# Two token groups share weight slices in rounds of seven, five and four instead of ten and six

## The chip, the cores and the metric

The kernel runs on one core of a Trainium2 chip. The metric is device time in microseconds (us), the median of several runs. A profile is one more execution, recorded by the hardware profiler; its span runs from the first to the last instruction. The engines are PE (matrix products), ACT (activations and copies with a scale), DVE (elementwise work and reductions), POOL (elementwise work) and SP, which here only issues DMAs. Each engine takes its own instructions in the order in which the program gives them.

## The reference

```python
k_p = k.reshape(B, H, Sp, 8, D).mean(axis=3)          # B 8, H 8, S 576, D 64, Sp 72
v_p = v.reshape(B, H, Sp, 8, D).mean(axis=3)
scores = np.matmul(q, k_p.transpose(0, 1, 3, 2)) / np.sqrt(D)
attn = softmax(scores)                                # max, exp, sum, as usual
x = np.matmul(attn, v_p)                              # as 4608 tokens of 512 channels
h = x @ w_in1                                         # 512 x 2048
x1 = (h * sigmoid(h)) @ w_out1                        # 2048 x 512
h = x1 @ w_in2
out = (h * clip(h + 3, 0, 6) / 6) @ w_out2
```

The weights come in double precision, as pairs of 32-bit words.

## The kernel before

**Groups and slices.** The 4608 tokens are 36 tiles of 128; four tiles make a group, so there are nine groups. The first weight matrix is cut into 16 slices of 128 hidden columns. A *slot* of the main loop (line 1008) is one product of a group with a slice (`h_mm`, line 628): 12 matmuls of 512 columns, three for each of four blocks, since a weight and an x value are each kept as a rounded head and a tail. The list `order` (line 837) says which group and slice a slot takes: slots 0 to 9 are group 0 with slices 0 to 9, slots 10 to 19 group 1 with the same slices, slots 20 to 25 and 26 to 31 the two groups with slices 10 to 15. From slot 32 on each group runs through all 16.

**Slices.** A slice's raw words are loaded by SP (line 119) and converted in four steps: *scale* on ACT (line 126), *bits*, three DVE instructions (lines 133, 136, 140), *head* on ACT (line 147), *tail* on DVE (line 152). The table `stages` says in which slot each step stands.

**Attention.** Group 0's tiles 0 to 3 are done ahead of slot 0. For a later tile the table `todo` places the steps: *scores* (PE, line 458, into two PSUM banks), *maxima* (DVE, lines 502 and 505), *exponentials* (ACT, line 512, eight of them, which also sum), *norm* (DVE, lines 529, 532, 533), then for group 1 *transposes* on PE (line 544) with two ACT copies out of PSUM (line 545), *weighted* (PE, line 592) and *split* of the result into head (ACT, line 608) and tail (DVE, line 609), which is the group's x. From group 2 on the transpose is three DVE instructions (line 566) and DMAs. In slots 0 to 9 group 1's tiles 4 to 7 pass through these steps, a tile every two slots, while one slice a slot is converted.

**The gate.** After a slot's product comes `silu`: tanh on ACT (line 641) and one DVE instruction (line 642), both in the next slot. Its store is issued by SP a slot later. The product's PSUM bank is free after it; `h_mm` takes turns over four banks, two of a pool `ps_h` and two called y0 and y1.

**Keys and values.** Batches 2 and up are loaded (lines 368, 376) in slots of their own (`kv_in`, from slot 6 on) and summed in eights by POOL. `summed_v` does this on PE (line 395) for two pairs of batch 1 in slots 0 and 1.

Of the kernel before, what the change touches and what calls it, by code (L numbers as in the profile page):

```python
# [27 lines left out]
def kernel(  # L28
# [14 lines left out]
    nc = tc.nc  # L43
# [78 lines left out]
    def split_scale(f):  # L122

        hw = w_raw[f][:, :, 1]
        mag = w_mag[f] = prep_tile("out", DM)
        nc.scalar.activation(mag, hw.bitcast(F32), AF.Copy, scale=2.0 ** -112)

    def split_bits(f):


        raw = w_raw.pop(f)
        bits = w_mag[f].bitcast(U32)
        nc.vector.tensor_scalar(
            out=bits, in0=bits, scalar1=3, scalar2=None, op0=ALU.logical_shift_left
        )
# [12 lines left out]

    def split_tail(f):

        t = w_sl[f]
        nc.vector.tensor_tensor(
            out=t[:, 1, :], in0=w_mag.pop(f), in1=t[:, 0, :].bitcast(F32), op=ALU.subtract
        )
        t = t.rearrange("p a (c f) -> p a c f", f=P)
        w_sl[f] = (t[:, 0], t[:, 1])
# [462 lines left out]
    def h_mm(g, f, m):  # L619
        ih, il = w_sl[f]  # L620
        xh, xl = xs[g]
        if m % 2:
            ps = ps_y.tile([P, GT], F32, tag=f"y{m // 2 % 2}", name="hps")
        else:
            ps = ps_h.tile([P, GT], F32, tag="h", name="hps")
        for n, (w, x) in enumerate(((ih, xh), (il, xh), (ih, xl))):
            for c in range(NKC):
                nc.tensor.matmul(  # L628
                    ps,
                    w[:, c, :],  # L630
                    shuffled(x[:, c, :]),
                    start=(c == 0 and n == 0),
                    stop=(c == NKC - 1 and n == 2),
                )
        return ps
# [197 lines left out]
            first_tile.setdefault(b, t)  # L833


    FIRST = 10
    order = [(0, f) for f in range(FIRST)] + [(1, f) for f in range(FIRST)]
    order += [(0, f) for f in range(FIRST, NF)] + [(1, f) for f in range(FIRST, NF)]
    order += [(g, f) for g in range(2, NG) for f in range(NF)]

    todo = {}
# [1 line left out]
    for t in range(TPG, NTILE):  # L843
        g, i = divmod(t, TPG)
        if g == 1:
            s, w = ((-1, 3), (1, 5), (3, 7), (5, 8))[i]
        elif g == 2:
            s, w = ((14, 25), (16, 26), (18, 28), (20, 29))[i]
        else:
            w = NF * (g - 1) + (4, 7, 10, 13)[i]  # L850
            s = w - 10
        start[t] = s
        jobs = [(s, "scores"), (s + 1, "soft"), (w, "weighted"), (w + 1, "split")]
        if g == 1:
            jobs += [(s + 2, "norm"), (s + 3, "probs" if i < TPG - 1 else "early")]
        else:
            jobs += [(s + 3, "norm"), (s + 3, "turn")]
        for n, what in jobs:
            if n >= 0:
                todo.setdefault(n, []).append((what, t))  # L860
# [4 lines left out]
            assert n not in kv_in  # L865
            kv_in[n] = (b, j)
    stages = {}
    for f in range(3, NF):
        n = f if f < FIRST else FIRST + 5 + 2 * (f - FIRST)
        for i, what in ((n - 5, "scale"), (n - 4, "bits"), (n - 3, "head")):  # L870
            if i >= 0:
                stages.setdefault(i, []).append((what, f))

    with tc.manual_schedule():
# [12 lines left out]
        def load_ahead(n):  # L887
            for _ in range(n):
                if ahead:
                    load_w(ahead.pop(0))  # L890
# [31 lines left out]
        for j in range(2, NPAIR):  # L922
            pool_v(1, j)
        load_q(TPG + 1)
        load_ahead(4)
        for t in range(2):
            scores(t, banks[t], 0)
        vps = bank(banks[3], 1)
# [46 lines left out]
        split_bits(1)  # L975
        split_scale(2)
        split_head(1)
        split_bits(2)
        split_tail(1)
        split_scale(3)  # L980
        split_head(2)
        split_bits(3)
        split_tail(2)
        split_scale(4)
        load_ahead(6)

        BEGIN = 20
# [17 lines left out]

        late_silu = []
        pv = {}
        for n, (g, f) in enumerate(order):
            if (g, f) == (NG - 1, 0):
                early.close()  # L1010
                open_ring()
            load_ahead(2)
            if n == 0:
                load_q(TPG + 2)
            if n >= BEGIN - 3:
                load_halves()
            if n in kv_in:
                load_k(*kv_in[n])
                load_v(*kv_in[n])
            for job in due.pop(n, ()):  # L1020
                job()
            while later:
                later.pop(0)()
            now = todo.get(n, ())
            if n == 0:
                ps = h_mm(g, f, n)
                scores(TPG)
            for what, t in now:
                if what == "split" and t < 2 * TPG:
                    split_x(t, pv.pop(t))  # L1030
                elif what == "norm" and t == 2 * TPG - 1:
                    norm(t, 2)
            for what, t in now:
                if what == "soft":
                    all_max(t)
            if late_silu:
                silu(*late_silu.pop())
            for what, t in now:
                if what == "split" and t >= 2 * TPG:
                    split_x(t, pv.pop(t))  # L1040
            for what, i in stages.get(n, ()):
                if what == "head":
                    split_head(i)
            for what, i in stages.get(n, ()):
                if what == "bits":
                    split_bits(i)
            for what, i in stages.get(n, ()):
                if what == "scale":
                    split_scale(i)
            resting = n == BEGIN + 3 if n < 2 * NF else n % NF in REST and n < (NG - 2) * NF  # L1050
            job = jobs.pop(0) if n >= BEGIN and not resting and jobs else None
            if job:
                job[0](job[2])
            for what, t in now:
                if what == "soft":
                    new_pr(t)
                    all_exps(t)
                elif what == "early":
                    probs_T(t, [(ps_y, "y2"), (ps_y, "y3")])
            if n:  # L1060
                ps = h_mm(g, f, n)
            late_silu.append((g, f, n, ps))
            if n == 0:
                vps = bank(banks[3], 1)
            if n < 2:
                summed_v(vps, 1, n)
            if n == 1:
                nc.scalar.activation(vp[1][:, :4 * D], vps[:SP, :4 * D], AF.Copy)
            for what, t in now:
                if what == "scores":  # L1070
                    scores(t)
                    if TPG < t + 2 < NTILE and t > TPG:
                        load_q(t + 2)
                elif what == "weighted":
                    pv[t] = weighted(t, A if t in (TPG + 2, TPG + 3) else [(ps_y, f"y{2 + t % 2}")])
            for what, t in now:
                if what == "norm" and t != 2 * TPG - 1:
                    norm(t, 2)
                elif what == "turn":
                    vector_T(t, n)  # L1080
                elif what == "probs":
                    probs_T(t, [(ps_y, "y2"), (ps_y, "y3")])
            for what, i in stages.get(n, ()):
                if what == "head":
                    split_tail(i)
            if job:
                job[1](job[2])
            if n - 3 in kv_in:
                pool_k(*kv_in[n - 3], nc.gpsimd)
                pool_v(*kv_in[n - 3])  # L1090
            if g == NG - 2 and f in (8, 10):
                next_wide(1)
            if g == NG - 1:
                if f < 2:
# [310 lines left out]
```

## Time and profile before

| | |
|---|---|
| median of 3 runs | 1515.35 us (1514.25 to 1515.46) |
| profiled execution | 1515.26 us, span 1513.5 us |
| PE busy | 1488.4 us, 98% of the span |
| DVE busy | 1239.5 us, 82% |
| ACT busy | 799.1 us, 53% |
| granted TensorE clock, mean | 0.996 of full speed |

PE is busy nearly throughout, so what can change is the rest, about 25 us in which it is idle, and the stretches in which its clock is halved.

### The profile page before, as it was taken

The numbers are of one execution on the slowest core, as the hardware profiler recorded it, in microseconds if no ns is written. First come the engines' busy times: TensorE is split into PE (matmuls) and PEld (weight loads), VectorE is DVE, ScalarE is ACT, GpSimd is POOL, SyncE is SP. The second block draws the span as 40 slices with busy tenths as digits, with TensorE's granted clock in tenths as the row PEclk, the third lists the DMA queues.
The fourth block names the chain that finished last, engine by engine and source line by source line (L and its number), as shares of the span: only waits on it lengthen the run. The fifth ranks groups of instructions, "written<-read, shape, count | busy, mean of one in ns | idle before, by whom it ended". The sixth has DMA issues, their size and how long they took to land.

```text
span 1513.5 us, 30723 instructions
## 1 busy us (share of the span) xinstructions
PE 1488.4 (98%) x11578; PEld 1418.1 (94%) x11578; DVE 1239.5 (82%) x1869; ACT 799.1 (53%) x1779; POOL 342.0 (23%) x389
## 2 busy tenths in 40 slices
PE   8899999999999999999999999999999999999998
PEld 7688888888888999999999999999999999999998
DVE  8879887888775898888988598888885877777776
ACT  5655564556544544444443566777676444444443
POOL 6163443443011000000000244555540000000000
PEclk9999999999999999999999999999999999999999
DMA  9567999899799955555559766556579954444440
GB/s 305 185 189 240 302 302 286 251 296 297 255 310 363 368 184 183 184 177 183 182 175 356 262 216 209 190 198 214 198 249 319 370 167 143 143 142 141 142 137 29
DMA packets 225460, 342.16 MB, mean 226 GB/s; under 512 B 16800, under 2 KB 157984, under 8 KB 225312
## 3 DMA queue, kind: packets, MB, share of 16 engines
q1 hardware_dynamic: 225312, 340.20, 67.6%
q8 instruction: 91, 1.49, 0.4%
q14 instruction: 57, 0.47, 0.1%
HBM read 194.90 MB, written 145.23 MB: 225 GB/s over the span
## 4 chain that ended last, share of the span: by engine, by line
PE 86%; DMA 6%; DVE 5%; issue 1%; ACT 1%; POOL 1%; SPq 0%; DVEq 0%; POOLq 0%; ACTq 0%
PE pl L821 22%; PE pl L805 22%; PE hps L628 20%; PE py L721 11%; PE pa L721 5%; PE ph L721 3%; DMA wraw<-in_moe_w_in_dram 2%; PE aps L592 2%; PE aps L458 2%; DMA stage<-in_v_dram 2%; DVE rs L1244 1%; DMA wst<-ws 1%; DMA x<-rs 1%; ACT pr L512 0%; DVE rw L218 0%
## 5 line engine op out<-in xcount | busy, mean ns | idle before, releaser
L628 PE MATMUL hps<-rx,whl 128*128 128x512 f32 x1728 | 389.7, 384 | 2.9 <-ACT rx L608 1.4
L628 PEld LDWEIGHTS hps<-rx,whl 128*128 128x128 f32 x1728 | 323.9, 190 | 51.5 <-issue 2.6
L805 PEld LDWEIGHTS pl<-rx,wst 128*128 128x128 f32 x3024 | 337.8, 192 | 0.1
L805 PE MATMUL pl<-rx,wst 128*128 128x256 f32 x3024 | 337.8, 275 | 0.0
L821 PE MATMUL pl<-wst,rx 128*128 128x256 f32 x3024 | 337.8, 275 | 0.0
L821 PEld LDWEIGHTS pl<-wst,rx 128*128 128x128 f32 x3024 | 337.8, 192 | 0.0
L223 POOL TENSOR_TENSOR rw<-rw 128x256 f32<-128x256 f32 x96 | 74.3, 781 | 577.6 <-DVE rw L218 555.1
L721 PE MATMUL py<-rx,wst 128*128 128x288 f32 x1152 | 152.5, 287 | 3.5 <-ACT rs L1308 1.9
L721 PEld LDWEIGHTS py<-rx,wst 128*128 128x128 f32 x1152 | 145.8, 190 | 4.1 <-ACT rs L1308 2.1
L642 DVE SCALAR_TENSOR_TENSOR rs<-rs,hps 128x512 f32<-128x512 f32 x144 | 97.7, 680 | 60.0 <-ACT rs L641 59.7
L791 ACT ACTIVATE rx<-ro 128x1024 fp32r<-128x1024 f32 x86 | 90.3, 1059 | 87.6 <-PE pl L805 35.7
L1121 DVE TENSOR_TENSOR rs<-rs,pl 128x512 f32<-128x512 f32 x90 | 61.7, 686 | 69.5 <-PE pl L821 47.2
L792 DVE TENSOR_TENSOR rx<-ro,rx 128x1024 fp32r<-128x1024 f32 x86 | 103.5, 1224 | 14.8 <-ACT rx L791 14.6
L512 ACT ACTIVATE pr<-aps,mxa 128x72 f32<-128x72 f32 x256 | 77.9, 331 | 55.8 <-DVE mxa L505 55.7
L641 ACT ACTIVATE rs<-hps 128x512 f32<-128x512 f32 x144 | 86.5, 610 | 39.2 <-PE hps L628 39.1
L1124 ACT ACTIVATE rs<-pl 128x512 f32<-128x512 f32 x36 | 21.5, 598 | 145.9 <-PE pl L821 76.2
L791 ACT ACTIVATE rx<-ra 128x1024 fp32r<-128x1024 f32 x70 | 73.4, 1059 | 47.3 <-PE pl L805 18.6
L214 ACT ACTIVATE rw<-rw 128x256 fp32r<-128x256 f32 x152 | 62.2, 419 | 64.9 <-POOL rw L223 31.7
L695 POOL TENSOR_TENSOR rx<-ro,rx 128x576 fp32r<-128x576 f32 x39 | 61.3, 1575 | 137.5 <-ACT rx L690 137.5
L792 DVE TENSOR_TENSOR rx<-ra,rx 128x1024 fp32r<-128x1024 f32 x70 | 83.4, 1219 | 9.9 <-ACT rx L791 9.8
L791 ACT ACTIVATE rx<-rb 128x1024 fp32r<-128x1024 f32 x63 | 66.1, 1058 | 44.7 <-PE pl L821 20.5
L218 DVE TENSOR_TENSOR rw<-rw 128x256 fp32r<-128x256 f32 x152 | 74.1, 497 | 10.6 <-ACT rw L214 10.3
(135 smaller groups left out, 2153.7 us busy)
## 6 DMA issues: line engine op xcount, KB each, us to landing
ws<-rw SPq DMA_DIRECT2D x152, 256.0 KB
wst<-ws SPq DMA_DIRECT2D x76, 512.0 KB
g<-rs SPq DMA_DIRECT2D x144, 256.0 KB
g<-rs SPq DMA_DIRECT2D x128, 288.0 KB
ro<-g SPq DMA_DIRECT2D x49, 512.0 KB
ra<-g SPq DMA_DIRECT2D x38, 512.0 KB
rb<-g SPq DMA_DIRECT2D x37, 512.0 KB
rw<-in_moe_w_out_dram SPq DMA_DIRECT2D x64, 256.0 KB
```

What stands on the lines that cost most here:

```text
L214: nc.scalar.activation(t[:, 0], mag, AF.Copy)
L218: nc.vector.tensor_tensor(out=t[:, 1], in0=mag, in1=t[:, 0].bitcast(F32), op=ALU.subtract)
L223: nc.gpsimd.tensor_tensor(out=out, in0=a, in1=b, op=op)
L512: nc.scalar.activation(p_t[t][:, a, i], s_t[t][a][:, i], AF.Exp, scale=ESCALE, bias=mx[:, h], accum_out=den_of(t)[:, h],)
L628: nc.tensor.matmul(ps, w[:, c, :], shuffled(x[:, c, :]), start=(c == 0 and n == 0), stop=(c == NKC - 1 and n == 2),)
L641: nc.scalar.activation(in_two(t), dealt(ps), AF.Tanh)
L642: nc.vector.scalar_tensor_tensor(out=in_two(t), in0=in_two(t), scalar=1.0, in1=dealt(ps), op0=ALU.add, op1=ALU.mult)
L721: nc.tensor.matmul(ps[j], w[:, j, a, c, :], shuffled(x[:, b, c, :]), start=(first and n == 0 and c == 0), stop=(n == 2 and c == 1), skip_g ...
L791: nc.scalar.activation(t[:, dd, 0], src, AF.Copy)
L792: nc.vector.tensor_tensor(out=t[:, dd, 1], in0=src, in1=t[:, dd, 0].bitcast(F32), op=ALU.subtract)
L805: nc.tensor.matmul(ps[:, c * HW:(c + 1) * HW], w[:, b, c * P:(c + 1) * P], shuffled(t[:, dd, a, i]), start=(dd == 0 and c == 0 and i == 0 ...
L821: nc.tensor.matmul(ps[:, c * HW:(c + 1) * HW], t[:, dd, a, i, c * P:(c + 1) * P], shuffled(w[:, b]), start=(dd == 0 and c == 0 and i == 0 ...
```

## The change

The rounds become seven, five and four slices: slots 0 to 6 and 7 to 13 are groups 0 and 1 with slices 0 to 6, slots 14 to 18 and 19 to 23 slices 7 to 11, slots 24 to 27 and 28 to 31 slices 12 to 15. Slots 0 to 6 get a body of their own, `opening`. In it a tile of group 1 starts every slot: its maxima and exponentials stand in slot 0, 1, 2 or 3, norm and transposes one slot later, weighted two and split three slots later. Slice n + 2 is converted in slot n; slices 7 to 15 follow two slots apart, as slices 10 to 15 did. Scores of tiles 4 and 5 and both value sums stand in slot 0. In slots 0 to 6 the products use only the two banks of `ps_h`; y0 and y1 take scores, y2 and y3 transposes and weighted results. For group 2, weighted of the first two tiles moves from slots 25 and 26 to slot 27.

```diff
-        if m % 2:
+        if m % 2 and m >= FIRST:
             ps = ps_y.tile([P, GT], F32, tag=f"y{m // 2 % 2}", name="hps")
...
-    FIRST = 10
-    order = [(0, f) for f in range(FIRST)] + [(1, f) for f in range(FIRST)]
-    order += [(0, f) for f in range(FIRST, NF)] + [(1, f) for f in range(FIRST, NF)]
+    FIRST, SECOND = 7, 12
+    order = []
+    for lo, hi in ((0, FIRST), (FIRST, SECOND), (SECOND, NF)):
+        order += [(g, f) for g in range(2) for f in range(lo, hi)]
...
-            s, w = ((14, 25), (16, 26), (18, 28), (20, 29))[i]
+            s, w = ((14, 27), (16, 27), (18, 28), (20, 29))[i]
...
-        split_bits(2)
         split_tail(1)
-        split_scale(3)
-        split_head(2)
-        split_bits(3)
-        split_tail(2)
-        split_scale(4)
...
+        def opening(n, f, now):
+
+            ps = h_mm(0, f, n)
+            if late_silu:
+                silu(*late_silu.pop())
+            late_silu.append((0, f, n, ps))
+            if n == 0:
+                scores(TPG, A)
+                scores(TPG + 1, B2)
+                load_q(TPG + 3)
+                vps1.append(bank(C, 1))
+                for j in range(2):
+                    summed_v(vps1[0], 1, j)
+            elif n == 1:
+                nc.scalar.activation(vp[1][:, :4 * D], vps1.pop()[:SP, :4 * D], AF.Copy)
...
+                if what == "norm":
+                    norm(t, 2)
...
+                if what == "split":
+                    split_x(t, pv.pop(t))
...
+                if what == "soft":
+                    all_max(t)
...
+                if what == "bits":
+                    split_bits(i)
...
+                if what == "soft":
+                    new_pr(t)
+                    all_exps(t)
...
+                if what == "probs":
+                    probs_T(t, C)
...
+                if what == "weighted":
+                    pv[t] = weighted(t, C)
...
+                if what == "scores":
+                    scores(t, B2 if t % 2 else A)
+                    load_q(t + 2)
...
+                if what == "head":
+                    split_head(i)
...
+                if what == "head":
+                    split_tail(i)
...
+                if what == "scale":
+                    split_scale(i)
```

How this moves instructions is seen on three engines. First ACT, from the exponentials of tile 5 (pr_87) to those of tile 6 (pr_86); L545 are the copies of tile 4's transposes. Before:

```order
L512 ACTIVATE pr_87,den<-aps,mxa 128x72 x8
L545 ACTIVATE ro<-aps 72x512 x2
L641 ACTIVATE rs<-hps 128x512
L147 ACTIVATE whl<-rw 128x512
L126 ACTIVATE rw<-wraw 128x512
L608 ACTIVATE rx<-aps 128x4x128
L641 ACTIVATE rs<-hps 128x512
L147 ACTIVATE whl<-rw 128x512
L126 ACTIVATE rw<-wraw 128x512
L512 ACTIVATE pr_86,den<-aps,mxa 128x72 x8
```

And after the change:

```order
L512 ACTIVATE pr_87,den<-aps,mxa 128x72 x8
L545 ACTIVATE ro<-aps 72x512 x2
L147 ACTIVATE whl<-rw 128x512
L126 ACTIVATE rw<-wraw 128x512
L641 ACTIVATE rs<-hps 128x512
L512 ACTIVATE pr_86,den<-aps,mxa 128x72 x8
```

One gate and one slice stand between two tiles instead of two of each, and the slice's head and scale now stand ahead of the gate's tanh.

The same stretch on DVE, from the gate ahead of tile 5's norm to tile 6's maxima. Before:

```order
L642 SCALAR_TENSOR_TENSOR rs<-rs,hps 128x512
L133 TENSOR_SCALAR rw<-rw 128x512
L136 SCALAR_TENSOR_TENSOR rw<-wraw,rw 128x512
L140 SCALAR_TENSOR_TENSOR rw<-wraw,rw 128x512
L529 TENSOR_SCALAR den<-den 128x8
L532 RECIPROCAL den<-den 128x8
L533 TENSOR_TENSOR pr_87<-pr_87,den 128x576
L152 TENSOR_TENSOR whl<-rw,whl 128x512
L609 TENSOR_TENSOR rx<-aps,rx 128x4x128
L502 TENSOR_REDUCE mxa<-aps 128x4 x2
L505 TENSOR_SCALAR mxa<-mxa 128x8
```

And after the change:

```order
L642 SCALAR_TENSOR_TENSOR rs<-rs,hps 128x512
L529 TENSOR_SCALAR den<-den 128x8
L532 RECIPROCAL den<-den 128x8
L533 TENSOR_TENSOR pr_87<-pr_87,den 128x576
L502 TENSOR_REDUCE mxa<-aps 128x4 x2
L505 TENSOR_SCALAR mxa<-mxa 128x8
L133 TENSOR_SCALAR rw<-rw 128x512
L136 SCALAR_TENSOR_TENSOR rw<-wraw,rw 128x512
L140 SCALAR_TENSOR_TENSOR rw<-wraw,rw 128x512
L152 TENSOR_TENSOR whl<-rw,whl 128x512
```

The bits and the tail of the slice have moved behind the maxima.

Last PE, from the scores of tile 6 before, and of tile 7 after the change; vp_84 are the values of batch 1. Before:

```order
L458 MATMUL aps<-kbd_81,qT 128x144 x4
L628 MATMUL hps<-rx,whl 128x512 x12
L544 MATMUL aps<-ident,pr_87 72x128 x8
L628 MATMUL hps<-rx,whl 128x512 x12
L592 MATMUL aps<-ro,vp_84 64x128 x8
```

And after the change:

```order
L458 MATMUL aps<-kbd_81,qT 128x144 x4
L628 MATMUL hps<-rx,whl 128x512 x12
L544 MATMUL aps<-ident,pr_86 72x128 x8
L592 MATMUL aps<-ro,vp_84 64x128 x8
L628 MATMUL hps<-rx,whl 128x512 x12
```

A product no longer stands between a tile's transposes and the next weighted product of the tile ahead of it.

## Rows read from the trace of the kernel before

**Rows 1.** The page, busy time of each engine: the row of PE.

```profile
PE 1488.4 (98%) x11578; PEld 1418.1 (94%) x11578; DVE 1239.5 (82%) x1869; ACT 799.1 (53%) x1779; POOL 342.0 (23%) x389
```

**Rows 2.** Windows: stretch, its length, busy time (instructions), clock, DMA share, GB/s.

```profile
28.70:79.00 50.30, 43.61 (x293) 36.02 (x293) 42.36 (x73) 29.99 (x101) 18.45 (x23) 0.93 0.62 221
79.00:94.60 15.60, 15.60 (x74) 13.70 (x73) 10.63 (x13) 6.13 (x10) 12.68 (x18) 1.00 0.45 126
```

**Rows 3.** Timeline of PE: start, us, operation, [idle before, releaser]; slots 0 to 14.

```profile
31.50 1.20 PE L458 MATMUL aps<-kbd,qT 128*64 128x144 f32 x16
...
42.19 2.54 PE L458 MATMUL aps<-kbd,qT 128*128 128x144 f32 x8 [2.63 <-ACT pr L512]
44.35 4.54 PE L628 MATMUL hps<-rx,whl 128*128 128x512 f32 x12
48.74 1.04 PE L544 MATMUL aps<-ident,pr 128*72 128x128 f32 x8
49.53 2.84 PE L628 MATMUL hps<-rx,whl 128*128 128x512 f32 x12
52.30 1.15 PE L592 MATMUL aps<-ro,vp 72*64 72x64 f32 x32
...
78.97 15.81 PE L628 MATMUL hps<-rx,whl 128*128 128x512 f32 x72
94.62 0.65 PE L458 MATMUL aps<-kbd,qT 128*128 128x144 f32 x4
```

**Rows 4.** Windows of 1 us; the third number from the end is the granted clock.

```profile
41.00:42.00 1.00, 0.00 (x0) 0.00 (x0) 0.93 (x3) 1.00 (x8) 0.00 (x0) 0.50 1.05 414
47.00:48.00 1.00, 1.00 (x4) 0.80 (x3) 1.00 (x3) 0.63 (x2) 0.00 (x0) 0.60 0.76 286
```

**Rows 5.** Timeline of ACT, from tile 5's first exponential to tile 6's.

```profile
49.09 0.32 ACT L512 ACTIVATE pr<-aps,mxa 128x72 f32<-128x72 f32 x1 [1.46 <-DVE mxa L505]
...
51.47 1.09 ACT L545 ACTIVATE ro<-aps 72x512 f32<-72x512 f32 x2
52.43 0.62 ACT L641 ACTIVATE rs<-hps 128x512 f32<-128x512 f32 x1
52.90 0.66 ACT L147 ACTIVATE whl<-rw 128x512 fp32r<-128x512 f32 x1
53.42 0.71 ACT L126 ACTIVATE rw<-wraw 128x512 f32<-128x512 f32 x1
53.99 0.63 ACT L608 ACTIVATE rx<-aps 128x512 fp32r<-128x512 f32 x1
...
59.08 0.32 ACT L512 ACTIVATE pr<-aps,mxa 128x72 f32<-128x72 f32 x1 [1.80 <-DVE mxa L505]
```

**Rows 6.** Timeline of DVE, the same stretch.

```profile
53.08 0.69 DVE L642 SCALAR_TENSOR_TENSOR rs<-rs,hps 128x512 f32<-128x512 f32 x1 [0.83 <-ACT rs L641]
53.68 0.42 DVE L133 TENSOR_SCALAR rw<-rw 128x512 uint32<-128x512 uint32 x1
...
55.66 0.16 DVE L529 TENSOR_SCALAR den<-den 128x8 f32<-128x8 f32 x1
...
56.77 0.69 DVE L152 TENSOR_TENSOR whl<-rw,whl 128x512 fp32r<-128x512 f32 x1
57.37 0.68 DVE L609 TENSOR_TENSOR rx<-aps,rx 128x512 fp32r<-128x512 f32 x1
57.97 0.81 DVE L502 TENSOR_REDUCE mxa<-aps 128x4 f32<-128x288 f32 x2
```

**Rows 7.** Timeline of DVE ahead of slot 1, while POOL still sums keys and values.

```profile
31.55 0.54 DVE L133 TENSOR_SCALAR rw<-rw 128x512 uint32<-128x512 uint32 x1
...
34.82 0.94 DVE L152 TENSOR_TENSOR whl<-rw,whl 128x512 fp32r<-128x512 f32 x1
```

**Rows 8.** Timeline of PE in slot 25, with its wait for slice 15's tail.

```profile
127.68 2.00 PE L628 MATMUL hps<-rx,whl 128*128 128x512 f32 x8 [0.66 <-DVE whl L152]
```

**Rows 9.** Timeline of SP: the second pair of keys of batch 2.

```profile
71.24 0.41 SPq L368 DMA_DIRECT2D stage<-in_k_dram  x1
```

More of the change, by code (lines that the diff above doesn't have):

```diff
@@ L845 @@
         if g == 1:
-            s, w = ((-1, 3), (1, 5), (3, 7), (5, 8))[i]
-        elif g == 2:
-            s, w = ((14, 25), (16, 26), (18, 28), (20, 29))[i]
+            if i > 1:
+                todo.setdefault(i - 1, []).append(("scores", t))
+            for n, what in ((i, "soft"), (i + 1, "norm"), (i + 1, "probs"), (i + 2, "weighted"), (i + 3, "split")):
+                todo.setdefault(n, []).append((what, t))
+            continue
+        if g == 2:
+            s, w = ((14, 27), (16, 27), (18, 28), (20, 29))[i]
         else:
@@ L853 @@
         jobs = [(s, "scores"), (s + 1, "soft"), (w, "weighted"), (w + 1, "split")]
[L854 to L857, printed above, removed]
+        jobs += [(s + 3, "norm"), (s + 3, "turn")]
         for n, what in jobs:
@@ L867 @@
     stages = {}
-    for f in range(3, NF):
-        n = f if f < FIRST else FIRST + 5 + 2 * (f - FIRST)
-        for i, what in ((n - 5, "scale"), (n - 4, "bits"), (n - 3, "head")):
+    for f in range(2, NF):
+        n = f - 2 if f < FIRST else FIRST - 1 + 2 * (f - FIRST)
+        for i, what in ((n - (1 if f < FIRST else 2), "scale"), (n - (f >= FIRST), "bits"), (n, "head")):
             if i >= 0:
@@ L924 @@
         load_q(TPG + 1)
-        load_ahead(4)
+        load_ahead(3)
+        load_q(TPG + 2)
+        load_ahead(1)
         for t in range(2):
@@ L1007 @@
         pv = {}
+        B2 = ((ps_y, "y0"), (ps_y, "y1"))
+        C = ((ps_y, "y2"), (ps_y, "y3"))
+        vps1 = []
+        def opening(n, f, now):
[12 more added lines that the diff above has]
+                nc.scalar.activation(vp[1][:, :4 * D], vps1.pop()[:SP, :4 * D], AF.Copy)
+            for what, t in now:
+                if what == "norm":
+                    norm(t, 2)
+            for what, t in now:
+                if what == "split":
+                    split_x(t, pv.pop(t))
+            for what, t in now:
+                if what == "soft":
+                    all_max(t)
+            for what, i in stages.get(n, ()):
+                if what == "bits":
+                    split_bits(i)
+            for what, t in now:
+                if what == "soft":
+                    new_pr(t)
+                    all_exps(t)
+            for what, t in now:
+                if what == "probs":
+                    probs_T(t, C)
+            for what, t in now:
+                if what == "weighted":
+                    pv[t] = weighted(t, C)
+            for what, t in now:
+                if what == "scores":
+                    scores(t, B2 if t % 2 else A)
+                    load_q(t + 2)
+            for what, i in stages.get(n, ()):
+                if what == "head":
+                    split_head(i)
+            for what, i in stages.get(n, ()):
+                if what == "head":
+                    split_tail(i)
+            for what, i in stages.get(n, ()):
+                if what == "scale":
+                    split_scale(i)
         for n, (g, f) in enumerate(order):
@@ L1024 @@
             now = todo.get(n, ())
[L1025 to L1032, printed above, removed]
+            if n < FIRST:
+                opening(n, f, now)
+                if n - 3 in kv_in:
+                    pool_k(*kv_in[n - 3], nc.gpsimd)
+                    pool_v(*kv_in[n - 3])
+                continue
             for what, t in now:
@@ L1038 @@
             for what, t in now:
-                if what == "split" and t >= 2 * TPG:
+                if what == "split":
                     split_x(t, pv.pop(t))
@@ L1057 @@
                     all_exps(t)
[L1058 to L1061, printed above, removed]
+            ps = h_mm(g, f, n)
             late_silu.append((g, f, n, ps))
[L1063 to L1068, printed above, removed]
             for what, t in now:
@@ L1071 @@
                     scores(t)
-                    if TPG < t + 2 < NTILE and t > TPG:
+                    if t + 2 < NTILE:
                         load_q(t + 2)
                 elif what == "weighted":
-                    pv[t] = weighted(t, A if t in (TPG + 2, TPG + 3) else [(ps_y, f"y{2 + t % 2}")])
+                    pv[t] = weighted(t, [(ps_y, f"y{2 + t % 2}")])
             for what, t in now:
-                if what == "norm" and t != 2 * TPG - 1:
+                if what == "norm":
                     norm(t, 2)
@@ L1080 @@
                     vector_T(t, n)
-                elif what == "probs":
-                    probs_T(t, [(ps_y, "y2"), (ps_y, "y3")])
             for what, i in stages.get(n, ()):
```

2 lines of the change are left out of this document (removed).

## Prediction

> **What bounds the kernel now.** I read the page first: PE is busy for 1488.4 of 1513.5 us [rows 1], so a change pays only where PE stands idle or runs at a lower clock. Windows over the slots that are rewritten come next: from 28.70 to 79.00, where group 0's first nine products and all attention of group 1 lie, PE is idle for 50.30 - 43.61 = 6.7 us and the mean clock is 0.93; from 79.00 to 94.60 it is idle for nothing [rows 2]. The timeline of PE shows the largest piece: the scores of tile 5 wait 2.63 us for ACT (the exponentials of tile 4, whose banks they take), and behind that wait they take 2.54 us and a product 4.54 us, where the next product takes 2.84 [rows 3]. The one-microsecond windows say why: the granted clock is 0.50 at 41, that is 1.2 GHz, and is back at 2.4 GHz within 47 to 48; its mean of 0.60 there puts the rise at about 47.8 [rows 4]. So the low clock held for another 5.6 us after PE had work again at 42.19, and cost about 4.54 - 2.84 + 2.54 - 1.20 = 3.0 us. Wait and clock together are 5.7 us, with some 4 us of smaller waits beside them. That is the most that the change could win in this stretch.
>
> What sets the pace of slots 2 to 9 is not PE but a ring through ACT and DVE. From tile 5's first exponential at 49.09 to tile 6's at 59.08 are 9.99 us, two slots [rows 5]. Its links, each taken from start to start: exponentials 2.38 (49.09 to 51.47), copies 0.96 (to 52.43), tanh to the gate on DVE 0.65 (to 53.08), gate 0.60, bits 1.98 (53.68 to 55.66), norm 1.11 (to 56.77), slice tail 0.60, split 0.60, maxima until the next exponential 1.11 (57.97 to 59.08) [rows 5, 6]. They add up to 9.99, with nothing left over: every link waits for the one ahead.
>
> **The change part by part.** The number of products, transposes, scores and conversions is the same, so PE's own work is the same. What changes is the ring.
>
> *The ring per tile.* A tile now takes one slot. On ACT the exponentials of tile t stand ahead of the copies of tile t - 1; then come head and scale of a slice, then tanh; on DVE gate, norm, maxima. From start to start: 2.38 + 0.96 + head 0.52 (52.90 to 53.42) + scale 0.57 (to 53.99) + 0.65 + 0.60 + 1.11 + 1.11 = 7.90 us [rows 5, 6]. Bits (1.98) now run on DVE beside the exponentials and cost nothing, which would end if exponentials and copies took less than maxima and bits. In slot 3 tile 4's split stands between norm and maxima: 8.50 us. A slot's work on PE is a product 2.77 (49.53 to 52.30), transposes 0.79 (48.74 to 49.53), weighted 1.15 and scores 1.20 or less [rows 3], 5.9 us in all. So PE waits some 2 to 3 us in every slot from 1 to 3, where before a wait of that length came once.
>
> *Where it starts.* Scores of tile 4 begin at 31.50 as before and take 1.20 [rows 3]. DVE then still has slice 1's tail; with 0.5 us for that (an estimate, part of the 0.94 that such a tail took [rows 7]) and 1.11 from maxima to exponential, the first exponential stands at 34.3. Slice 2's bits follow on DVE while POOL still sums; there they took 34.82 - 31.55 = 3.27 us against 1.98 [rows 6, 7]. With maxima done at 34.1 they end at about 37.4; head, scale, tanh, gate, norm and maxima follow: 37.4 + 0.52 + 0.57 + 0.65 + 0.60 + 1.11 + 1.11 = 42.0 for tile 5. Tile 6 starts at 42.0 + 7.9 = 49.9, tile 7 at 58.4.
>
> *How it ends.* Tile 7's exponentials end at 60.8, tile 6's copies at 61.7. Head, scale and tanh give 63.5; gate, norm and tile 5's split 65.8, when tile 7 can be transposed. From here PE is the one waited for: transposes and one of the two copies 0.79 + 0.48, weighted of tile 6 1.1, product of slot 5 2.8, weighted of tile 7 1.1, product of slot 6 2.8 [rows 3, 5]. Slot 7, group 1's first product, starts at 74.8.
>
> *Against before.* Products that follow one another take (94.62 - 78.97) / 6 = 2.61 us [rows 3]. At 94.62 tile 8's scores follow slot 14's product in both kernels. After the change eight products lie between slot 7's start and that point, so no time is won or lost if slot 7 starts at 94.62 - 8 x 2.61 = 73.8. It starts 1.0 us later. The ring wins 2.63 us of wait in slot 1 and loses as much in each of three slots, against the smaller waits of before; and two products fewer are there to fill them.
>
> *The clock.* Tile 4's norm ends 1.1 us ahead of tile 5's start, at 40.9; transposes, scores and slot 2's product keep PE busy until 45.7. It waits for tile 5's norm (48.8), transposes for 0.8 us, and waits again, since tile 4's weighted product goes into the bank out of which tile 5's first copy is taken: 49.9 + 2.38 + 0.48 = 52.8. A wait of 2.63 us brought the low level before [rows 3, 4], so these two of over 3 us do too. With 5.6 us at half speed from 52.8 on, as there, weighted, scores and product (5.1 us of work) end at 60.7 instead of 57.9. Tile 6's transposes then end just after tile 7's exponentials, behind which their copies queue on ACT anyhow: the ring waits 0.4 us. The bounds are 0 (the clock is back 3 us earlier) and 1.8 (it comes back only at 61.5, and transposes end at 62.8). I take 0.4, since the 5.6 us are those of the row.
>
> *What follows.* Slots 11 to 22 convert slices in the same slots as before, beside group 2's softmax. The wait of 0.66 us for slice 15's tail in slot 25 [rows 8] goes, since slice 15 is first used in slot 27 now. Part of it comes back in the four banks, which DVE frees at its own pace: between 0 and 0.66 won, I take 0.4. Weighted of tiles 8 and 9 in slot 27 leaves slots 28 to 31 for four splits: nothing, since group 2's first product comes in slot 32; without that room one split, 1.2 us on two engines.
>
> *The queues.* SP now loads tile 6's q between slices and tiles 7 to 9 in slots 0 to 2; slices 6 and up come up to 1.3 us later, but slice 6 is needed in slot 3 instead of slot 2 and slice 7 only in slot 14. Batch 2's second pair of keys, at 71.24 [rows 9], queues behind the stores of two gates, which end near 72.5 now: 1.3 us later, as slot 14 is, and POOL with it. Nothing, unless it slips past the scores of tile 9 in slot 16.
>
> *Sum.* 1.0 + 0.4 - 0.4 = 1.0 us on the profiled 1515.26 us (span 1513.5 and 1.8 around it), which lies 0.1 us under the median of the three runs: **1516.3 us**. About 0.2%, 3.0 us, is what a measurement of this kernel can tell from no change, so this is "the same".
>
> **The rivals.**
>
> *The low clock stays or comes back* (slower). If PE is at half speed after 65.8, nothing hides it: transposes, two weighted products and two products there are 8.5 us of work, all on the path. One more low stretch as in [rows 4] costs the 3.0 us that it cost there, and the first may cost its bound of 1.8 instead of 0.4: 1516.3 + 3.0 + 0.7 = about 1520. For it: three waits of 3 us in a row, each longer than the one that brought the low level. Against it: the third is filled if the product ahead of it runs slowly. It decides if the clock is not back by 62. The Trainium skill ("TensorE: Matmul & The Clock Gate", HAM oscillation) tells of a kernel in which every burst after a long wait starts at the low rate anew; by that each of the three waits would bring it, as this rival has it. The trace agrees for the one wait of 2.63 us; of waits in a row it shows nothing.
>
> *The waits close* (faster). PE's work from 28.70 to slot 7, without waits, is what it was busy until 79.00 less two products and the low clock's price: 43.6 - 5.5 - 3.0 = 35.1 us [rows 2], so slot 7 could start at 63.8, 10 us earlier. DVE's work in a slot, gate, norm, maxima, bits, tail and split, is at most 6.0 us, and ACT's is less: neither forbids a slot of about 6 us. If copies and maxima found their operands without the ring's turns, half of it would come, about 1510 us. Against it: each engine takes its instructions in order, and the same kind of sum gave before's 9.99 us exactly.
>
> *Slots 14 to 25 gain more than the sum has*: the 0.66 us and, with DVE freed earlier, more of the waits in that stretch: at 1 us over the sum the time is 1515.3, as before. For it: DVE has slices 8 and 9 ahead of slot 11, so none is pressed. Against it: slots 11 to 22 hold the same work on DVE as before.
>
> **How the numbers follow.** Forecast, with the third rival as its lower half: 0.62, between 1514.5 and 1518.4. Low clock: 0.26, 1518 to 1522. Waits close: 0.12, 1505 to 1512. The range takes in the forecast and most of the slow case, and leaves 2 in 10 out, mostly on the fast side: 1512.5 to 1520.5. Faster by over 0.2% (under 1512.3): 0.12, the last case. Slower (over 1518.4): 0.27, the clock case and a little more. The same: 0.61.
>
> **What would show it.** In the changed profile the first exponentials of tiles 4 to 7 should stand near 34.3, 42.0, 49.9 and 58.4; PE should wait about 3 us ahead of tile 5's transposes, again ahead of tile 4's weighted product, and once more, or less if the clock is low, ahead of tile 5's; the granted clock should be 0.50 from about 48 to 58; slot 7's product should begin near 75 and tile 8's scores near 96. The wait on slice 15's tail should be gone. Tiles less than 7 us apart would prove the ring wrong, and slot 7 before 71 the forecast; a clock of 0.50 after 62 would prove the first rival right.

## The result, and the profile after

The changed kernel takes 1523.99 us (median of 6 runs, 1522.07 to 1527.47) beside 1515.49 us for the kernel before in the same job (6 runs, 1514.25 to 1517.38): a ratio of 1.0056, interval 1.0043 to 1.0069. It is slower by 8.5 us where 1.0 was forecast, and above the top of the range. The profiled execution took 1522.07 us with a span of 1520.3.

The opening first. Timeline of PE in the changed kernel, slots 0 to 3 (start, us, operation, in brackets the idle time before it and its releaser):

```profile
28.98 2.86 PE L628 MATMUL hps<-rx,whl 128*128 128x512 f32 x12 [1.36 <-ACT rx L608]
31.77 2.38 PE L458 MATMUL aps<-kbd,qT 128*64 128x144 f32 x24
...
42.30 1.04 PE L544 MATMUL aps<-ident,pr 128*72 128x128 f32 x8 [2.06 <-DVE pr L533]
...
44.06 2.85 PE L628 MATMUL hps<-rx,whl 128*128 128x512 f32 x12
50.12 1.04 PE L544 MATMUL aps<-ident,pr 128*72 128x128 f32 x8 [3.21 <-DVE pr L533]
54.05 1.97 PE L592 MATMUL aps<-ro,vp 72*64 72x64 f32 x32 [2.89 <-ACT ro L545]
55.95 2.29 PE L458 MATMUL aps<-kbd,qT 128*128 128x144 f32 x8
57.87 3.12 PE L628 MATMUL hps<-rx,whl 128*128 128x512 f32 x12
```

and of ACT, the first exponentials of tiles 4 to 7:

```profile
35.20 0.32 ACT L512 ACTIVATE pr<-aps,mxa 128x72 f32<-128x72 f32 x1 [2.58 <-DVE mxa L505]
...
43.12 0.32 ACT L512 ACTIVATE pr<-aps,mxa 128x72 f32<-128x72 f32 x1 [2.54 <-DVE mxa L505]
...
51.01 0.32 ACT L512 ACTIVATE pr<-aps,mxa 128x72 f32<-128x72 f32 x1 [2.86 <-DVE mxa L505]
...
59.50 0.32 ACT L512 ACTIVATE pr<-aps,mxa 128x72 f32<-128x72 f32 x1 [2.83 <-DVE mxa L505]
```

The distances are 7.92, 7.89 and 8.49 us; the sum had 7.7 (42.0 - 34.3), 7.9 and 8.5. The waits of about 3 us stand where they were put. The start is off, 0.9 us late, 0.27 of which slot 0 itself is late, and the first distance, by another 0.2. Tile 8's scores start at 96.70, where before has 94.62 [rows 3].

Windows of both kernels from 131 us on, that is from slot 25 or 26 (columns as in [rows 2]). Changed:

```profile
131.00:200.00 69.00, 62.81 (x398) 53.45 (x397) 56.08 (x117) 34.69 (x122) 30.03 (x45) 0.95 0.86 265
200.00:400.00 200.00, 199.61 (x1173) 171.01 (x1172) 162.34 (x353) 110.45 (x409) 80.74 (x121) 1.00 0.90 286
```

Before:

```profile
131.00:200.00 69.00, 68.81 (x437) 59.01 (x436) 60.83 (x130) 38.51 (x143) 30.11 (x46) 1.00 0.93 294
200.00:400.00 200.00, 198.22 (x1167) 169.32 (x1167) 163.68 (x350) 108.46 (x405) 77.89 (x116) 1.00 0.89 282
```

From 131 to 200 PE now idles for 69.00 - 62.81 = 6.19 us (0.19 before) and the mean clock is 0.95 (1.00 before). The large loss is thus behind slot 25, not in the rewritten opening. The timeline of PE there:

```profile
104.51 0.51 PE L458 MATMUL aps<-kbd,qT 128*128 128x144 f32 x2 [0.75 <-POOL kbd L385]
...
138.82 1.97 PE L592 MATMUL aps<-ro,vp 72*64 72x128 f32 x32
140.72 2.86 PE L628 MATMUL hps<-rx,whl 128*128 128x512 f32 x12
149.77 1.98 PE L592 MATMUL aps<-ro,vp 72*64 72x128 f32 x16 [6.19 <-DVE rx L609]
151.67 3.99 PE L628 MATMUL hps<-rx,whl 128*128 128x512 f32 x12
...
156.52 1.15 PE L458 MATMUL aps<-kbd,qT 128*64 128x144 f32 x16
```

At 138.82 stand the weighted products of tiles 8 and 9, at 149.77 that of tile 10, and it is released by a split. ACT and DVE say which:

```profile
145.38 0.32 ACT L512 ACTIVATE pr<-aps,mxa 128x72 f32<-128x72 f32 x1 [2.90 <-DVE mxa L505]
...
148.23 1.13 ACT L608 ACTIVATE rx<-aps 128x512 fp32r<-128x512 f32 x2
```

```profile
149.03 1.28 DVE L609 TENSOR_TENSOR rx<-aps,rx 128x512 fp32r<-128x512 f32 x2
```

The line `pv[t] = weighted(t, [(ps_y, f"y{2 + t % 2}")])` gives tiles 8 and 10 the same bank, y2. It comes free with the first of the two tails at 149.03, and that stands in slot 28, as the product does that needs it, behind tile 12's exponentials. Before, two slots lay between them:

```profile
129.60 1.09 PE L592 MATMUL aps<-ro,vp 72*64 72x128 f32 x16
...
133.42 1.09 PE L592 MATMUL aps<-ro,vp 72*64 72x128 f32 x16
...
140.80 1.09 PE L592 MATMUL aps<-ro,vp 72*64 72x128 f32 x16
...
145.77 1.18 PE L458 MATMUL aps<-kbd,qT 128*64 128x144 f32 x16
```

Tile 10's weighted product, at 140.80, had no wait. Behind the wait the granted clock is low, in windows of one microsecond (clock third from the end):

```profile
149.00:150.00 1.00, 0.23 (x2) 0.24 (x4) 1.00 (x3) 1.00 (x3) 0.00 (x0) 0.50 0.95 194
...
153.00:154.00 1.00, 1.00 (x4) 0.73 (x4) 0.93 (x4) 0.00 (x0) 0.00 (x0) 0.50 1.06 390
154.00:155.00 1.00, 1.00 (x6) 0.89 (x5) 0.97 (x4) 0.00 (x0) 0.00 (x0) 1.00 1.08 397
```

0.50 is 1.2 GHz. Weighted and product take 1.98 and 3.99 instead of 1.09 and 2.86, 2.0 us. Wait and clock are 8.2 us; tile 13's scores come at 156.52 instead of 145.77, 10.75 late. In the span 6.8 are left: from 200 to 400 PE idles 1.78 us before and 0.39 now, and from 800 to 850 only the profile of before, of all twelve, shows a clock below 1.00 (0.97; PE is idle for 1.90 us there, 0.93 now). The last are some 2.5 us by estimate (3% of 50 us for the clock, 0.97 of idle time), which no row ties to the change.

### The profile page after: what moved, and what is told of

The parts are those of the page before. It is cut to its first block, busy times and chain, and to the rows that moved or that the text cites. A ratio compares the mean times of both kernels' runs of the same rounds, so it can differ in the third digit from the quotient of the medians.

```text
span 1520.3 us, 30720 instructions
## 1 busy us (share of the span) xinstructions
PE 1487.0 (98%) x11578; PEld 1418.2 (93%) x11578; DVE 1239.1 (82%) x1869; ACT 801.5 (53%) x1779; POOL 341.4 (22%) x389
## 3 DMA queue, kind: packets, MB, share of 16 engines
q8 instruction: 91, 1.49, 0.4%
## 4 chain that ended last, share of the span: by engine, by line
PE 87%; DVE 5%; issue 1%; ACT 1%; DMA 1%; POOL 0%; SPq 0%; DVEq 0%; ACTq 0%
PE pl L821 22%; PE pl L805 22%; PE hps L628 21%; PE py L721 11%; PE pa L721 5%; PE ph L721 3%; PE aps L592 2%; PE aps L458 2%; DVE rs L1282 1%; DMA x<-rs 1%; DVE rw L218 1%; DVE rs L642 0%; DVE rw L194 0%; DVE rs L1350 0%; DVE rw L191 0%
## 5 line engine op out<-in xcount | busy, mean ns | idle before, releaser
L792 DVE TENSOR_TENSOR rx<-rb,rx 128x1024 fp32r<-128x1024 f32 x63 | 75.9, 1230 | 5.9 <-ACT rx L791 5.8
```

Of the source, the lines that this page charges most:

```text
L792: nc.vector.tensor_tensor(out=t[:, dd, 1], in0=src, in1=t[:, dd, 0].bitcast(F32), op=ALU.subtract)
```

## The experiments

Ratios are to the kernel before in the same job (its medians there: 1514.19 to 1515.49 us). The stretch ahead of slot 0, which most of these kernels share, ends at different times in different executions (last section), so places in a profile are compared from slot 0's start, and times by medians. Even so a place is not exact: late_weighted_alone has the opening of the kernel before, and the second column differs by 1.3 us between the two; four kernels share the changed kernel's opening (changed, rounds_7_3_6, weighted_10_11_later, other_banks), and theirs spans 67.00 to 68.09.

| | slot 0 | tile 8's scores, after it | tile 13's scores, after it | median us | ratio, interval |
|---|---|---|---|---|---|
| before | 28.71 | 65.91 | 117.06 | 1515.49 | 1 |
| changed | 28.98 | 67.72 | 127.54 | 1523.99 | 1.0056, 1.0043 to 1.0069 |
| late_weighted_alone | 31.82 | 67.19 | 124.02 | 1523.82 | 1.0063, 1.0046 to 1.0080 |
| rounds_7_3_6 | 33.81 | 67.00 | 118.93 | 1518.53 | 1.0025, 1.0016 to 1.0035 |
| weighted_10_11_later | 29.86 | 68.09 | 124.67 | 1522.17 | 1.0051, 1.0033 to 1.0069 |
| other_banks | 31.89 | 67.28 | 119.56 | 1521.37 | 1.0040, 1.0025 to 1.0055 |
| norm_ahead_of_gate | 33.94 | 65.56 | 125.95 | 1522.49 | 1.0058, 1.0038 to 1.0078 |
| rounds_7_3_6_norm_ahead | 33.50 | 64.72 | 117.14 | 1514.51 | 0.9997, 0.9989 to 1.0006 |
| maxima_first_tail_later | 30.58 | 62.19 | 114.14 | 1511.04 | 0.9979, 0.9971 to 0.9988 |
| and_keys_earlier | 28.89 | 62.55 | 112.41 | 1511.83 | 0.9985, 0.9976 to 0.9995 |
| fillers | 28.43 | 71.45 | 129.02 | 1527.06 | 1.0088, 1.0072 to 1.0104 |
| keys_earlier_alone | 29.23 | 68.29 | 128.13 | 1522.65 | 1.0050, 1.0032 to 1.0068 |

**The late part.** *late_weighted_alone*: the kernel before with one line of the change.

```diff
-            s, w = ((14, 25), (16, 26), (18, 28), (20, 29))[i]
+            s, w = ((14, 27), (16, 27), (18, 28), (20, 29))[i]
```

> The kernel before with one line of the change: weighted of tiles 8 and 9 in slot 27 instead of 25 and 26. Bank theory (tile 10's weighted product in slot 28 takes bank y2, which tile 8's split frees in the same slot, so PE must wait until ACT and DVE have caught up with it): a wait of 5 to 7 us on PE ahead of tile 10's weighted product, with the clock at half speed behind it, 1521 to 1524 us. Rival (the wait comes from the opening, which leaves DVE late): without the opening nothing is late, 1515 to 1517 us.

1.0063. Its PE row in slot 28:

```profile
149.19 1.98 PE L592 MATMUL aps<-ro,vp 72*64 72x128 f32 x16 [5.42 <-DVE rx L609]
151.10 3.88 PE L628 MATMUL hps<-rx,whl 128*128 128x512 f32 x12
```

The same wait and the same low clock, without any of the new opening. This line alone costs as much as the whole change.

*rounds_7_3_6*: the changed kernel, with the two products back in slots 25 and 26, for which group 0 must be through by slot 25.

```diff
-    FIRST, SECOND = 7, 12
+    FIRST, SECOND = 7, 10
...
-            s, w = ((14, 27), (16, 27), (18, 28), (20, 29))[i]
+            s, w = ((14, 25), (16, 26), (18, 28), (20, 29))[i]
```

> The changed kernel with rounds of seven, three and six slices, so that group 0 ends in slot 25 as before, and weighted of tiles 8 and 9 in slots 25 and 26 as before. Bank theory: the 6.2 us wait is gone, what stays is the opening (1.8 us) and the two waits behind it (some 2 us, of which part is hidden later): 1517 to 1519.5 us. Rival (the opening is to blame for all): 1522 to 1525 us.

1.0025. Tile 10's product follows without a wait, as it did before:

```profile
140.62 1.09 PE L592 MATMUL aps<-ro,vp 72*64 72x128 f32 x16
...
148.00 1.09 PE L592 MATMUL aps<-ro,vp 72*64 72x128 f32 x16
```

Of the 0.56% more than half is gone. What is left goes with the opening: with the same rounds, and only the opening's order on DVE changed, the ratio is 0.9997 (rounds_7_3_6_norm_ahead, below). The two losses do not add up: 0.63% for the late line alone and 0.25% here are more than the 0.56% of both.

*weighted_10_11_later*: the changed kernel, with one slot of room.

```diff
-            s, w = ((14, 27), (16, 27), (18, 28), (20, 29))[i]
+            s, w = ((14, 27), (16, 27), (18, 29), (20, 30))[i]
```

> The changed kernel with weighted of tiles 10 and 11 one slot later (29 and 30), so that a slot lies between tile 8's split and the next use of its bank. Bank theory: the wait shrinks by about one slot, from 6.2 to 3 or 4 us, and the low clock behind it may go: 1518 to 1521 us, unless group 2's first product in slot 32 now waits for tile 11's split instead. Rival (the wait is for work on DVE and not for the bank): the wait moves with the product and the time stays at 1523 to 1525 us.

The wait shrinks from 6.19 to 3.61 us, by about one product, but the low clock behind it stays, now over the scores too, and the time, above what was expected, is not told from the changed kernel's. (Its profile also has waits of 2.35 and 0.48 us at tile 9's scores, to which keys_earlier_alone comes back, and tile 13's scores stand ahead of tile 11's product in this order, so its last column is not quite like the others.)

```profile
152.77 1.98 PE L592 MATMUL aps<-ro,vp 72*64 72x128 f32 x16 [3.61 <-DVE rx L609]
154.53 2.13 PE L458 MATMUL aps<-kbd,qT 128*64 128x144 f32 x16
156.60 3.90 PE L628 MATMUL hps<-rx,whl 128*128 128x512 f32 x12
```

*other_banks*: the changed kernel in its own order, with other banks in four places.

```diff
-        if m % 2 and m >= FIRST:
+        if m % 2 and m >= FIRST and m not in (29, 31):
...
-                    pv[t] = weighted(t, [(ps_y, f"y{2 + t % 2}")])
+                    pv[t] = weighted(t, [(ps_y, f"y{t % 2 if t in (10, 11) else 2 + t % 2}")])
```

> The changed kernel, with the same order on every engine; only the banks differ: the second products of tiles 10 and 11 go to banks y0 and y1 instead of y2 and y3, and the products of slots 29 and 31 to the pair h. Theory (TensorE waits in slot 28 for the bank that tile 8's split frees, and for nothing else): it goes on in slot 28 and stands about 1.2 us before slot 29's product and 0.4 us before tile 11's second product, for banks that the gates of slots 27 and 28 free; tile 13's scores 4 to 6 us earlier than in the changed kernel, 1518 to 1521 us. Rival (ScalarE and VectorE are simply late there and TensorE must wait for them in the same slot whatever bank it takes): the 6.2 us are found again at another instruction of slots 28 to 30, 1523 to 1524.

```profile
144.84 1.09 PE L592 MATMUL aps<-ro,vp 72*64 72x128 f32 x16
147.37 2.83 PE L628 MATMUL hps<-rx,whl 128*128 128x512 f32 x12 [1.43 <-DVE rs L642]
150.52 1.09 PE L592 MATMUL aps<-ro,vp 72*64 72x128 f32 x16 [0.33 <-DVE rs L642]
...
157.09 2.83 PE L628 MATMUL hps<-rx,whl 128*128 128x512 f32 x12 [1.58 <-DVE rs L642]
```

Tile 10's product no longer waits, the two waits expected are there (1.43 and 0.33), the clock is 1.00 throughout, and tile 13's scores come 8.0 us earlier from slot 0, 6.4 of which lie between tile 12's scores and them. The wait is the bank's. The borrowed banks are then missed: 1.58 and 0.33 us more, which were not expected. The time, 1521.37, lies just above what was expected, and its interval overlaps the changed kernel's: that the wait goes with the bank is shown, a gain in time is not. (From slot 0 to the end its profile takes 1485.9 us beside 1491.3, one profile each.)

**The opening.** *norm_ahead_of_gate*: the changed kernel, in `opening` with the factors and maxima on DVE ahead of the gate of the slot before.

```diff
             ps = h_mm(0, f, n)
-            if late_silu:
-                silu(*late_silu.pop())
+            gate = list(late_silu)
+            late_silu.clear()
...
                 if what == "soft":
                     all_max(t)
+            if gate:
+                silu(*gate.pop())
```

> The changed kernel with another order in slots 0 to 6: on DVE norm and maxima stand ahead of the gate, so that tanh, head and scale on ACT are no longer links of the ring. Ring theory: tiles start 5 to 6.5 us apart instead of 7.9, PE waits less than 1 us per slot there, no low clock in slots 2 and 3, tile 8's scores near 91 instead of 96.7; the wait of tile 9's scores for the keys of batch 2 grows from 0.75 to 3 to 5 us and gives part back; 1518 to 1521 us, since tile 10's wait stays. Rival (each tile's steps need 8 us whatever the order): tiles 7.5 us or more apart, 1523 to 1525 us.

Exponentials start 5.85, 6.86 and 8.04 us apart, two of the three further than expected, since the slice's tail, which waits for ACT's head, still stands ahead of the factors (norm) on DVE; in the third distance the maxima also wait 0.49 and 0.50 us for scores, which PE computes at the low clock (2.29 us instead of 1.15). PE still waits 2.19 and 2.60 us, where under 1 was expected. The tail:

```profile
50.60 0.69 DVE L152 TENSOR_TENSOR whl<-rw,whl 128x512 fp32r<-128x512 f32 x1 [1.44 <-ACT whl L147]
51.21 0.17 DVE L529 TENSOR_SCALAR den<-den 128x8 f32<-128x8 f32 x1
```

Tile 8's scores come 2.2 us earlier from slot 0, but the wait in slot 28 follows all the same (6.19 us); the wait for batch 2's keys, expected to grow to 3 to 5 us, is 0.84; the time cannot be told from the changed kernel's.

*rounds_7_3_6_norm_ahead*: both edits.

> The changed kernel with two edits together: rounds of seven, three and six with the second products of tiles 8 and 9 in slots 25 and 26, as in the kernel before, and in slots 0 to 6 the factors and the maxima ahead of the gate on VectorE. Theory (two separate losses, the late bank y2 in slot 28 and the opening's ring): both gains add, tile 8's scores 65.5 us after slot 0's product, no wait over 1 us at tile 10's second product, 1516 to 1517.5 us. Rival (the late part loses the same whatever the opening gives, because the waits are one budget of lead): 1518.5, as with the rounds alone. Second rival (the low clock was the opening's real loss): also no gain, 1518 to 1519.

0.9997: as before, and better than expected. With the late wait gone, what the opening gives is kept; with it, as the run above shows, it is not.

*maxima_first_tail_later*: on top of that, a tile's maxima ahead of the factors of the tile before, and a slice's tail in the next slot, behind both.

```diff
             for what, t in now:
-                if what == "norm":
-                    norm(t, 2)
-            for what, t in now:
                 if what == "soft":
                     all_max(t)
+            for what, t in now:
+                if what == "norm":
+                    norm(t, 2)
+            for what, i in stages.get(n - 1, ()):
+                if what == "head":
+                    split_tail(i)
```

> The kernel of the run above with two more moves on VectorE in slots 0 to 6: a tile's maxima stand ahead of the factors of the tile before, and a slice's tail stands in the next slot, behind both. Then no exponential waits for the tile before it but on ScalarE itself, and the slot is as long as TensorE's work (43.6 us in 7 slots and tile 4's scores, 6.2 a slot). Theory (the opening's loss is the ring through VectorE): first exponentials 6.0 to 6.5 apart, PE waits under 1 us each, tile 8's scores 62 to 63 us after slot 0, but the keys of batch 2, whose loads and sums keep their slots, wait longer at tile 9's scores (0.75 before, 1 to 2.5 now); 1512.5 to 1515 us. Rival (TensorE at low clock, or the loads, set the pace): spacing stays at 6.9 to 8, 1516 to 1517.

```profile
36.96 0.32 ACT L512 ACTIVATE pr<-aps,mxa 128x72 f32<-128x72 f32 x1 [2.73 <-DVE mxa L505]
...
42.15 0.31 ACT L512 ACTIVATE pr<-aps,mxa 128x72 f32<-128x72 f32 x1
...
47.26 0.36 ACT L512 ACTIVATE pr<-aps,mxa 128x72 f32<-128x72 f32 x1
...
55.18 0.32 ACT L512 ACTIVATE pr<-aps,mxa 128x72 f32<-128x72 f32 x1 [2.37 <-DVE den L529]
```

The exponentials of tiles 5 and 6 start 5.2 and 5.1 us behind the ones ahead of them and wait for nothing but ACT; the third distance is 7.9, behind two waits of PE (1.90, and 0.81 for tile 7's queries, still on their way by DMA) and a low clock (0.50 from 53 to 55). Tile 8's scores come 62.19 us after slot 0, 5.5 earlier than in the changed kernel. 1511.04 us, 0.9979: better than expected, and this version beats both kernels. A first round of seven can pay; the change's order on DVE did not let it. Whether the same order on DVE would do as much for the kernel before, with rounds of ten and six, was not run.

*and_keys_earlier*: the kernel above with batch 2's keys two slots earlier (`n = 4 + 2 * j` in `kv_in`).

> The kernel of the run above with the keys and values of batch 2 loaded and summed two slots earlier. Theory: the wait for them at tile 9's scores (0.75 us in the changed kernel) goes, and no other takes its place: 0.5 to 2 us under the run above, 1511.5 to 1514. Rival (the loads of the slices and of group 1's queries stand behind those of the keys on SP's queue, and their splits come late): the wait moves to a product in slots 7 to 12, same time as the run above.

The wait at tile 9's scores (0.81 there) is gone, and waits of 1.16 and 1.49 us for splits stand in slots 4 and 5. The medians cannot be told apart, as the rival said, though the new waits are in the opening, not behind it. From slot 0 to the end its profile is 3.7 us shorter than the one above (1478.1 beside 1481.8), which the medians do not bear out: a difference of that size between two single profiles shows no gain.

*keys_earlier_alone*: the same line in the changed kernel.

> The changed kernel with the keys and values of batch 2 loaded and summed two slots earlier. Theory (their lateness costs the 0.75 us wait at tile 9's scores and the rest of the late part is untouched): that wait is gone, the wait of about 6 us in slot 28 stays and takes up what was gained, 1523 to 1524. Rival (what is gained ahead of slot 16 is kept to the end): 1522.5 to 1523.2, and its profile measured from slot 0's product is 0.7 us or more shorter.

Neither: the keys are there in time, and the wait grows, from 0.75 to 1.04 and 0.48 us:

```profile
104.88 0.73 PE L458 MATMUL aps<-kbd,qT 128*128 128x144 f32 x4 [1.04 <-POOL stage L402]
106.10 0.73 PE L458 MATMUL aps<-kbd,qT 128*128 128x144 f32 x4 [0.48 <-POOL stage L403]
```

The releaser in these rows does other work: the sums of batch 2's keys had ended at 95.2. The starts fit ACT instead, where tile 8's exponentials, whose two banks these scores take, run from 103.46 to 105.85 (99.03 to 101.4 in the changed kernel). They are late by DVE: of the 4.4 us, 0.8 were there at 83 us, and 3.4 come from the bits of two slices, which take 4.15 and 4.04 us (from 83.42 and from 90.18) instead of 2.16 and 2.62. POOL's sums run beside them in both kernels; but in the changed kernel the longer instructions there are POOL's. Timelines of DVE and POOL, the first of the two slices, changed kernel:

```profile
83.92 0.83 DVE L140 SCALAR_TENSOR_TENSOR rw<-wraw,rw 128x512 uint32<-128x512 uint32 x1
```

```profile
84.09 1.76 POOL L402 TENSOR_TENSOR stage<-stage 72x512 f32<-72x512 f32 x1
```

and keys_earlier_alone:

```profile
85.89 1.68 DVE L140 SCALAR_TENSOR_TENSOR rw<-wraw,rw 128x512 uint32<-128x512 uint32 x1
```

```profile
83.06 1.26 POOL L402 TENSOR_TENSOR stage<-stage 72x512 f32<-72x512 f32 x1
```

The earlier load is not shown to be the cause. weighted_10_11_later, in which keys and bits stand as in the changed kernel, has the same: 4.15 and 4.26 us for these two slices, tile 8's exponentials at 105.20 and the waits of 2.35 and 0.48 us for them; and and_keys_earlier, with the earlier load, has 2.19 and 3.03 and no wait. What the earlier load does by itself is left open by this one profile.

*fillers*: the changed kernel with unused matmuls ahead of the transposes in slots 1 to 4, `probs_T(t, C, warm=12)`.

> The changed kernel with twelve matmuls of 288 columns, which compute nothing that is used, ahead of each tile's transposes in slots 1 to 4, so that part of TensorE's waits there is filled. Theory (the ring through VectorE and ScalarE sets the slot, the low clock of 51 to 58 us costs at most its half microsecond): the granted clock of that stretch is higher, first exponentials of tiles 6 and 7 at most 0.6 us earlier, the time 0 to 1 us under the changed kernel's, 1523 to 1524. Rival (the low clock costs the opening more, some 2 us by the products of slots 3 and 4): tile 8's scores 1.5 us or more earlier, 1521.5 to 1522.5.

Slower than the changed kernel, which neither theory had. Where PE would not have waited, the fillers cost their own 1.6 us:

```profile
61.23 1.63 PE L444 MATMUL aps<-rx 128*128 128x288 f32 x12
```

The wait that they could not fill, 2.95 us ahead of tile 4's weighted product, stays, and the clock falls at 52 to 53 all the same. What the low clock by itself costs in the opening is therefore left open by this run.

## Why the prediction was wrong

- *"Weighted of tiles 8 and 9 in slot 27 leaves slots 28 to 31 for four splits: nothing."* **This step failed.** It asked when group 2's x is needed, and not when the banks of the products are: tile 10's product takes tile 8's bank. 6.19 us of wait and 2.0 of low clock stood there; one line in the kernel before brings them (1.0063), other banks or earlier products take the wait away. The "one split, 1.2 us" named as its price for want of room had the size wrong too: the split begins on ACT at 148.23, 7.5 us after the products that it takes up have ended on PE (140.72), so PE lost its lead over ACT and DVE, which the wait of 6.19 us puts at more than two products.
- *Keys of batch 2, "nothing, unless it slips past the scores of tile 9"*: they slipped past, 0.75 us (0.66 in rounds_7_3_6, 0.41 in other_banks). Whether an earlier load alone would win that back is open.
- *The ring*: right to 0.02 us in the two distances that it gives (7.89 and 8.49), and the waits came where forecast. The start was 0.9 us late: beside slot 0's 0.27, slice 1's tail ended 0.4 later than its estimate (it took 1.32 us, where 0.5 were put behind the scores), and maxima took 0.2 more. The first distance was 7.92 instead of 7.7. Slot 7 is late with them: slot 6's product stands at 73.28, so slot 7 begins one product of 2.6 later, near 75.9 where 74.8 was forecast.
- *The opening's clock*: 0.50 from about 51.6 to 58.4 (the windows at its ends have 0.80 and 0.79), where the sum had 52.8 and the last part "about 48 to 58". Opening and clock together were to cost 1.4 us; tile 8's scores are 1.8 late from slot 0, which one pair of profiles can't tell from 1.4 (67.00 to 68.09 with this opening, 65.91 and 67.19 with the one before).
- *The wait on slice 15's tail*: gone, as forecast. That any of it was kept at the end is hidden by the wait in slot 28.
- *Rivals*: "the low clock stays or comes back" had the right side, but neither the size (1518 to 1522 us; its sum adds 0.7 for a bound that is 1.4 above the value taken, so 1520.7 and not 1520) nor the place: the clock came back behind slot 28, as a consequence. "Slots 14 to 25 gain more" did not come: the scores of tiles 9 and 11 wait 0.75, and 1.16 and 0.45 us there (none, and 0.41 and 0.45 before). "The waits close" did not come by the change, but maxima_first_tail_later, with rounds of seven, three and six, comes near the 1510 that it named, and by the means it named.

## What to carry to other kernels

When a step is moved later, list everything that its successors free, PSUM banks first: the question is not only who needs its result, but who needs its place. Count the room in slots between a release and the next taker on the engine that runs ahead, since there a release in the same slot costs the whole lead. And where a ring sets the pace, the order of the instructions within a slot on one engine can be worth more than the rounds around it (with the same rounds of seven, three and six, the ratio went from 1.0025 to 0.9979).

## What the runs showed of the hardware

DVE and POOL can lengthen each other's instructions, and either may be the one that pays: beside POOL's sums line 140, which has two SBUF inputs, took 1.68 us in keys_earlier_alone and 0.83 in the changed kernel, where POOL's L402 took 1.76 instead of 1.26. It changes between executions too: up to slot 28 weighted_10_11_later has the changed kernel's code, and the bits of the same two slices took 4.15 and 4.26 us there instead of 2.16 and 2.62. What decides between the two was not tested. The Trainium skill ("GPSIMD Engine Reference", Specifications) says that the two engines share their interfaces to SBUF, with contention where a DVE instruction has two SBUF inputs. The trace agrees for line 140, with twice the time.

The stretch ahead of slot 0 differs from execution to execution: slot 0 starts between 28.43 and 33.94 us in the twelve profiles. In a late one, rounds_7_3_6, PE waits there for POOL's values 2.47 us (0.71 in the profile of before), and the granted clock is low behind it:

```profile
20.00:25.00 5.00, 2.53 (x21) 1.91 (x20) 4.66 (x8) 2.87 (x12) 4.69 (x7) 0.75 0.90 350
25.00:30.00 5.00, 5.00 (x34) 4.14 (x33) 2.14 (x4) 1.67 (x3) 4.41 (x9) 0.57 1.03 256
```

That is as large as most differences studied here and would explain much of the 4 to 8 us by which runs of one kernel differ, which was not tested; a profile's span alone cannot be compared.

The length of a wait did not tell by itself whether the clock falls. A wait of 2.06 us in the changed kernel was followed by a product at full speed (2.85 us), one of 2.63 before by a slow one [rows 3], and in maxima_first_tail_later waits of 1.90 and 0.81 with a weighted product between them by one of 3.81. The same wait of 1.36 us ahead of slot 0's product was followed by 2.86 us for it in the changed kernel and by 4.54 in fillers. The Trainium skill ("TensorE: Matmul & The Clock Gate", HAM oscillation) tells of a kernel in which every burst behind a long wait starts at the low rate. The trace agrees for the 6.19 us in slot 28.
